# Splitting the first small load of a bf16 layer-scale kernel in two

## The chip, the core and the metric

The kernel runs on one core of one Trainium2 chip. The time is device microseconds of that core, the median over several executions. Smaller is better.

## What is computed

The reference adds a scaled tensor to another one; the scale is one vector over the last dimension:

```python
B, S, D = 1024, 16, 512          # x, y: (B, S, D) bf16; gamma: (D,) bf16
def reference(x, y, gamma):
    return x + gamma * y
```

x, y and the output have 16,384 rows of 512 elements, 1 KB each. So 33.55 MB are read and 16.78 MB written, with one multiply and one add for each element.

## The kernel before

The 16,384 rows are laid over the 128 partitions, 128 rows to each. `BLOCKS = [8, 60, 60]` cuts these 128 rows into three blocks; within a block every partition's rows lie one after the other in memory, so one load or store of a block moves 8 or 60 KB for each partition in one piece (`rows_of`). All of y stays on chip in `y_sb`; the multiply and the add both write in place there, and the stores read from it. x has a smaller buffer, `x_sb`, of 75 rows: the last number of an x load says where in it the rows go. Rows 68 to 127 of x are put at row 15, over rows 23 to 67, and rows 0 to 7 at row 0, over rows 8 to 15, so these two loads wait until the adds that used the rows before are done.

The order of the work is written out by hand in three lists:

- `SP`: the loads of x and y, as (tensor, first row, end row, place). SyncE issues them in this order on one DMA queue (called q1 in the profile). `EARLY` moves the first two loads to the head of the program.
- `ACT`: gamma and the three stores, issued by ScalarE on another queue (q10). The stores are for rows 8 to 67, 68 to 127, and 0 to 7.
- `DVE`: what VectorE does. `PIECES = [8, 15, 45, 60]` cuts the 128 rows into pieces 0 to 3, and ('m', c) multiplies piece c of y by gamma (L170), ('a', c) adds piece c of x to it (L179). Piece 0 is the small block, pieces 1 and 2 together are rows 8 to 67, piece 3 is rows 68 to 127.

The function `ring` walks through a queue's list and puts a wait on the adds in front of an item that needs one. A wait holds everything behind it in the same list.

gamma is spread over the partitions at the start: TensorE multiplies a column of ones with the gamma row (L144), VectorE copies the product from PSUM (L146), and every multiply reads that copy.

No store starts while the big loads run. `RELEASE` names the load of rows 68 to 127 of x. TensorE waits for it and then raises two semaphores, one for ScalarE's first store and one for VectorE's add of piece 3:

```python
_take(s_load[RELEASE], 16, nc.tensor)
nc.tensor.sem_inc(s_go, 1)
nc.tensor.sem_inc(s_rel, 1)
```

A store also waits until the pieces of its rows are added (`s_add`, counted in the order of the adds in `DVE`). In front of a multiply or an add VectorE takes the semaphores of the loads that its piece needs and that it has not taken yet (`need`).

Of the kernel before, what the change touches and what calls it, by code (L numbers as in the profile page):

```python
# [9 lines left out]


SP = [
    ('y', 0, 8),
    ('y', 8, 68),
    ('x', 8, 68, 0),
    ('y', 68, 128),
    ('x', 68, 128, 15),
    ('x', 0, 8, 0),
]
ACT = [('g',), ('s', 8, 68), ('s', 68, 128), ('s', 0, 8)]  # L20
# [2 lines left out]

RELEASE = ('x', 68, 128, 15)

DVE = [('m', 0), ('m', 1), ('m', 2), ('a', 2), ('a', 1), ('m', 3), ('a', 3), ('a', 0)]
MULT, ADD = mybir.AluOpType.mult, mybir.AluOpType.add


# [6 lines left out]
def kernel(  # L36
# [49 lines left out]
    s_add, s_go, s_rel, s_end, s_out = sem("s_add"), sem("s_go"), sem("s_rel"), sem("s_end"), sem("s_out")  # L86
    added = [a for kind, *a in DVE if kind == "a"]
    order = {a[0]: k for k, a in enumerate(added)}
# [74 lines left out]

    for kind, *args in DVE:
        c = args[0]
# [58 lines left out]
```

## Time and profile before

| what | value |
|---|---|
| time, median of 3 runs (lowest to highest) | 119.93 us (119.85 to 120.49) |
| span of the profiled execution | 118.5 us |
| VectorE busy | 70.1 us (59%) |
| TensorE busy | 0.6 us |
| load queue q1 | 33.55 MB, 65.8% of 16 engines' span |
| gamma and store queue q10 | 16.78 MB, 32.7% |
| multiply of piece 0, add of piece 0 | 2.29 us, 2.28 us |
| multiply, add of piece 3 | 16.16 us, 16.16 us |

The span is counted from the first to the last instruction of the profiled execution; the time takes in a little more. L33 is the helper `_take`, so a wait that ends with DVEq L33 is one for a semaphore of VectorE's own list. In the lines of the profile DVE is VectorE, PE is TensorE, SPq and ACTq are the DMA issues of SyncE and ScalarE. A line of the timeline has the start, the length up to the end of the last instruction merged into it, engine, line, operation, output and input, how many there are, and in brackets how long the engine stood idle before it and what ended that. A line of a stretch has its window and length, then the busy time of PE, PEld, DVE and POOL, the granted clock, the share of the DMA engines, and GB/s.

### The profile page before, as it was taken

The page shows a single profiled execution, that of the slowest core. Times are in us where ns is not written, and L with a number is a line of the kernel's source. Part 1 is how long each engine was busy: PE and PEld are TensorE (multiplying, and loading weights), DVE is VectorE, ACT ScalarE, POOL GpSimd, SP SyncE. Part 2 cuts the span into 40 slices and gives each one's busy share as a digit, 9 for nine tenths or more (in the row PEclk, how much of TensorE's full clock was granted, in tenths as well). Part 3 has the DMA queues.
Part 4 walks back from the last instruction along what each step waited for, and adds up shares of the span by engine and source line. Part 5 has one row for each costly group of instructions (what it writes and reads, how often), then busy time and mean ns, then how long its engine had stood idle before and what let it go on. Part 6 is the DMA issues. An engine that isn't in the chain of part 4 may idle for free. (4 is left out here: it accounts for less than half of the span.)

```text
span 118.5 us, 81 instructions
## 1 busy us (share of the span) xinstructions
PE 0.6 (0%) x1; PEld 0.1 (0%) x1; DVE 70.1 (59%) x10; POOL 0.2 (0%) x4
## 2 busy tenths in 40 slices
PE   0001000000000000000000000000000000000000
PEld 0000000000000000000000000000000000000000
DVE  0005400299999399999499999469999950000000
POOL 0000000000000000000000000000000000000000
DMA  5999779779779779978977977897797797797787
GB/s 180 506 602 394 332 332 663 332 332 663 332 332 663 332 332 601 394 332 352 643 332 332 663 332 332 384 633 332 332 663 332 332 663 332 332 663 332 332 365 321
DMA packets 1298, 50.33 MB, mean 425 GB/s; under 512 B 145, under 2 KB 146, under 8 KB 146
## 3 DMA queue, kind: packets, MB, share of 16 engines
q1 hardware_dynamic: 864, 33.55, 65.8%
q10 hardware_dynamic: 434, 16.78, 32.7%
HBM read 33.56 MB, written 16.78 MB: 425 GB/s over the span
## 5 line engine op out<-in xcount | busy, mean ns | idle before, releaser
L170 DVE TENSOR_TENSOR y_sb<-y_sb,gamma_sb 128x4096 bf16<-128x4096 bf16 (+3 forms) x4 | 34.7, 8689 | 11.9 <-DVEq L33 11.9
L179 DVE TENSOR_TENSOR y_sb<-x_sb,y_sb 128x23040 bf16<-128x23040 bf16 (+3 forms) x4 | 34.6, 8688 | 4.5 <-DVEq L33 4.5
L146 DVE CAST gamma_sb<-gamma_ps 128x512 bf16<-128x512 f32 x1 | 0.7, 690 | 7.9 <-DVEq L33 7.9
L141 DVE MEMSET ones_row<- 1x128 bf16 x1 | 0.2, 165 | 2.0 <-PEq L49 2.0
L144 PE MATMUL gamma_ps<-gamma_row,ones_row 1*128 1x512 bf16 x1 | 0.6, 581 | 9.3 <-PEq L33 9.3
L144 PEld LDWEIGHTS gamma_ps<-gamma_row,ones_row 1*128 1x128 bf16 x1 | 0.1, 97 | 9.3 <-issue 9.3
L208 POOL MEMSET const-bfloat16-1.0<- 128x1 bf16 x1 | 0.1, 102 | 0.0
L208 POOL MEMSET const-uint8-127<- 128x1 uint8 x1 | 0.1, 102 | 0.0
L208 POOL MEMSET const-float32-0.0<- 128x1 f32 x1 | 0.1, 99 | 0.2 <-issue 0.2
L208 POOL MEMSET const-float32-1.0<- 128x1 f32 x1 | 0.1, 99 | 0.0
## 6 DMA issues: line engine op xcount, KB each, us to landing
y_sb<-in_y_dram SPq DMA_DIRECT2D x2, 7680.0 KB, 39.8
x_sb<-in_x_dram SPq DMA_DIRECT2D x2, 7680.0 KB, 31.5
out_dram<-y_sb ACTq DMA_DIRECT2D x2, 7680.0 KB, 21.0
y_sb<-in_y_dram SPq DMA_DIRECT2D x1, 1024.0 KB, 4.8
x_sb<-in_x_dram SPq DMA_DIRECT2D x1, 1024.0 KB, 22.3
out_dram<-y_sb ACTq DMA_DIRECT2D x1, 1024.0 KB, 22.1
gamma_row<-in_gamma_dram ACTq DMA_DIRECT2D x1, 1.0 KB
```

The costliest lines, as they stand in the source:

```text
L141: nc.vector.memset(ones_row, 1.0).then_inc(s_ones, 1)
L144: nc.tensor.matmul(gamma_ps, ones_row, gamma_row, start=True, stop=True).then_inc(s_ps, 1)
L146: nc.vector.tensor_copy(out=gamma_sb, in_=gamma_ps).then_inc(s_dve, 1)
L170: nc.vector.tensor_tensor(out=yt, in0=yt, in1=g, op=MULT).then_inc(s_dve, 1)
L179: nc.vector.tensor_tensor(out=yt, in0=xt, in1=yt, op=ADD).then_inc(s_add, 1)
L208: nc = _bacc.Bacc("TRN2", target_bir_lowering=False, num_devices=1)
```

## The change

The load of rows 0 to 7 of y, the first of all, is cut in two. Rows 0 to 3 stay in first place; rows 4 to 7 go behind the last big load, in front of the small load of x. The aim is that rows 8 to 67 of y, with which the long work of VectorE begins, reach the chip earlier. Since the whole of piece 0 is then on chip only near the end of the loads, its multiply goes from first place in VectorE's list to the last but one.

```diff
 SP = [
-    ('y', 0, 8),
+    ('y', 0, 4),
     ('y', 8, 68),
     ('x', 8, 68, 0),
     ('y', 68, 128),
     ('x', 68, 128, 15),
+    ('y', 4, 8),
     ('x', 0, 8, 0),
 ]
-DVE = [('m', 0), ('m', 1), ('m', 2), ('a', 2), ('a', 1), ('m', 3), ('a', 3), ('a', 0)]
+DVE = [('m', 1), ('m', 2), ('a', 2), ('a', 1), ('m', 3), ('a', 3), ('m', 0), ('a', 0)]
```

## The prediction

> **What bounds the kernel now.** I read the slices of the page first, then the same stretch summed over the whole stream, then the timeline and the chain of waits. The page's slices show which resource is never idle:
>
> ```profile
> DVE  0005400299999399999499999469999950000000
> ...
> DMA  5999779779779779978977977897797797797787
> ...
> DMA packets 1298, 50.33 MB, mean 425 GB/s; under 512 B 145, under 2 KB 146, under 8 KB 146
> ...
> q1 hardware_dynamic: 864, 33.55, 65.8%
> q10 hardware_dynamic: 434, 16.78, 32.7%
> ```
>
> VectorE is idle for whole stretches; the DMA row never falls to 0, and the two queues together fill 98.5% of 16 engines' span. q1 is the load queue (SyncE issues it), q10 gamma and the stores (ScalarE). The sevens are no gaps: bytes and time are booked in coarse packets of up to 61,440 B. Over the stream from its first packet to its last the share is
>
> ```profile
> 1.00:118.20 117.20, 0.58 (x1) 0.10 (x1) 70.12 (x10) 0.00 (x0) 1.00 1.00 429
> ```
>
> The last two columns are the share of the DMA engines, 1.00, and 429 GB/s. The trace's packet records say it packet by packet: a 61,440 B packet takes 2.267 us, an 8,192 B one 0.309 us, the next one on the same engine starts within 0.05 us, and no longer gap is found on any engine between 1.03 us (first packet) and 118.11 us (last end). So the kernel lasts as long as its bytes, plus a start of about 1.8 us and a tail of 0.4 us for the last landing. The timeline shows where the order of work could leave a hole:
>
> ```profile
> 0.00 0.85 SPq L130 DMA_DIRECT2D y_sb<-in_y_dram  x2
> 1.90 0.33 SPq L127 DMA_DIRECT2D x_sb<-in_x_dram  x1
> ...
> 11.02 2.29 DVE L170 TENSOR_TENSOR y_sb<-y_sb,gamma_sb 128x4096 bf16<-128x4096 bf16 x1 [0.26 <-DVEq L33]
> 23.10 16.23 DVE L170 TENSOR_TENSOR y_sb<-y_sb,gamma_sb 128x7680 bf16<-128x7680 bf16 x2 [9.79 <-DVEq L33]
> 41.36 16.23 DVE L179 TENSOR_TENSOR y_sb<-x_sb,y_sb 128x23040 bf16<-128x23040 bf16 x2 [2.04 <-DVEq L33]
> 53.55 4.39 SPq L127 DMA_DIRECT2D x_sb<-in_x_dram  x2
> 59.40 16.16 DVE L170 TENSOR_TENSOR y_sb<-y_sb,gamma_sb 128x30720 bf16<-128x30720 bf16 x1 [1.81 <-DVEq L33]
> 77.76 19.02 ACTq L133 DMA_DIRECT2D out_dram<-y_sb  x3
> 78.05 18.36 DVE L179 TENSOR_TENSOR y_sb<-x_sb,y_sb 128x30720 bf16<-128x30720 bf16 x2 [2.49 <-DVEq L33]
> ```
>
> The reader is to see that each VectorE stage ends with a wait of 1.8 to 9.8 us for a load, so VectorE follows the loads, and that its work is issued to the queues ahead of need. The load of x rows 68 to 127 is issued at 53.55, 5.0 us before its first packet runs (58.55). The second store is issued at 94.24, 3.0 us before the first store's packets end (97.27). The chain that ended last says the same by what it lacks:
>
> ```profile
> by line: issue 12.0%; DVE y_sb L179 3.5%
> ...
> 79.94 14.18 issue
> 94.13 2.28 DVE y_sb L179
> ```
>
> It goes back only from the last store's issue through the last two adds; the 22 us behind 96.4 are stores, which it doesn't count as work.
>
> **What the Trainium skill says.** "DMA: Bandwidth & Descriptors", section "Where 436 GB/s comes from", gives 435.2 GB/s for the 16 ports together. The trace agrees: 61,440 B in 2.267 us is 27.1 GB/s per engine, 433.6 for sixteen. Only fewer bytes, or less start and tail, would make the kernel faster, and the change touches no byte count. The same page, "Queues, rings and completion order", says that an engine round-robins between queues packet by packet. The trace shows one case: the 1 KB packet of gamma (q10, issued at 1.91) ran at 6.56 between two 61,440 B packets of q1, and its semaphore write came one such packet later, at 8.87. The same page, "Latency and other measured facts", prices an HBM access at 0.2 us on average; the trace of before has no store-to-load change on an engine, so this is used below as a price. "VectorE: DVE Perf Modes", section "The perf-mode tier table", has bf16 tensor_tensor at 1224 ns for 2048 elements, so a moved instruction keeps its price; here 4096 elements take 2.29 us.
>
> **The change, part by part.**
> *The load stream.* One load of 8 packets of 8,192 B per engine becomes two of 8 packets of 4,096 B. From the two packet sizes: 53,248 B cost 1.958 us, so 27.19 B per ns and 7.7 ns fixed. A 4,096 B packet is then 0.158 us by that estimate, 16 of them 2.53 us against 8 x 0.309 = 2.47: +0.06 us. One semaphore write more per engine is 0.009 us. Both lie on the stream, and so on the end: +0.07.
> *The start.* Before, first packets begin at 1.03 to 1.83 and all end by 2.28, the earliest taking 1.04 us: cold latency. Then come seven more, until 4.20. Now eight short ones take 8 x 0.151 = 1.21 us less, so with the 0.07 of the next item they end from 3.06 on, and rows 8 to 67 of y must be queued by then. That load is issued at 0.43; with the first load's delay of 1.03 to 1.83 it is there at 1.46 to 2.26, so 0.8 us to spare. If the cold latency ends with one packet in flight, it now hides 0.15 us less data: 0 to 0.15, I take 0.07.
> *VectorE.* Multiply 0 (2.29 us) leaves a place where VectorE then idled 9.79 us, which hid it, and goes between add 3 and add 0, with a wait for two y loads that landed long before. All big loads land 1.14 us earlier (1.21 less 0.07): rows 8 to 67 of y at 21.8 for 22.96, the last big x load at 76.3 for 77.41. Add 3 starts near 76.9 and ends near 93.1, multiply 0 at 95.4, add 0 at 97.7, against 96.42. Behind multiply 0 only add 0 is queued, and for that waits only the last store, issued near 97.8. It is next in its queue when the second store ends, at about 115.5, and needs some 1.4 us from issue to packets (77.76 to 79.14 for the first store): 16 us of room. Cost 0. The second store is issued at 93.1 in place of 94.2; its room grows.
> *The hand-over from loads to stores.* Stores are released when the last big x load lands. Before, 2.47 us of x rows 0 to 7 ran behind that load: the first store was issued at 77.76, and its packets began at 79.14, on each engine straight after the last load packet. Now 1.27 us of y rows 4 to 7 run there too. The first store is issued near 76.6 and is ready from 77.6 (1.03 later) to 78.0 (1.4 later), with 4 to 6 load packets and semaphore writes left on q1. Taken in turn with 61,440 B store packets, x rows 0 to 7 land after about 79.2 + 5 x 2.27 + 0.35 = 90.9 (0.35: from a last packet to its landing, as 4.20 to 4.54); at worst, with 7 left, 95.4. Add 0 needs them at 95.4, and has 16 us beyond. So no engine idles, and the order of packets leaves the sum as it is. What is unknown is whether an engine loses time where a load follows a store. Lower bound: nothing, as at the load-to-store change (0.01 us). Upper: 5 x 0.2 = 1.0 us by the skill's HBM price, or 5 x 0.73 = 3.7 us with the cold latency of the first packet (1.04 less 0.31). I take 0.02 each, 0.1 in all: packets of one queue follow each other without any exposed latency, so reads are asked for ahead. Gamma points there too: with the store's 1.4 us it was ready at 3.3, yet three 8 KB packets and one big one of q1 went first. If that is look-ahead, there are hardly any alternations at all.
> Sum: 0.07 + 0.07 + 0 + 0.1 = +0.24; half of the last two is guesswork, so 119.93 + 0.2 = 120.1 us.
>
> **Rivals.**
> A, slower by the mixed queues: each of 5 alternations exposes a read, 1.0 us by the price in place of the 0.1 taken, so 121.0; up to 123.7 with the cold latency. For it: the kernel has never mixed small loads with stores in this trace, and the end is set by every lost engine nanosecond. Against: the look-ahead above.
> B, slower by a hole at the start: if rows 8 to 67 of y were ready only at 4.20, where they start now, 1.1 us are lost: 120.1 + 1.1 = 121.2. For it: nothing in the trace shows them ready earlier. Against: issue times and the first load's delay put them at 2.3.
> C, faster: data earlier on VectorE and an earlier store shorten the end. VectorE does get its inputs 1.14 us sooner, and if that reached the end the time would be 118.8. Against: the stores have no hole to close, the first follows the loads at once and the second is queued 3 us ahead. Known savings end at a shorter cold start, some 0.3 us, so this case would need something that the trace doesn't show.
>
> **How the numbers follow.** The forecast (a stream as long as before, 119.9 to 120.4) has 0.70. A has 0.17 and B 0.05, C 0.08, of which 0.07 pass the 0.5% bound of 0.6 us. Slower by over 0.5% means above 120.53: A and B, all but a little, 0.23 with the tail of the forecast; same 0.70. The range of 119.7 to 121.2 holds the forecast with the spread of the runs before (119.85 to 120.49), B, and A by the price; left out are C and A's high end.
>
> **What would show it.** Right: packets of 4,096 B near 0.158 us, no gap on an engine at 3.1 us, the big y load landing near 21.8, the release near 76.3, first store issued near 76.6, x rows 0 to 7 landing as late as 91, multiply 0 after add 3 without a wait, and the last packet near 118.3. Wrong: a hole at 3.1 us (B), load packets that take clearly over 0.31 us or follow a store with a gap (A), or a last store that starts after a hole because add 0 came too late, past 114.

## The result, and the profile after

The changed kernel takes 121.01 us (120.98 to 121.26, 6 runs) beside 119.94 us before: a ratio of 1.0088, with a 95% interval of 1.0068 to 1.0109. It is slower by 1.1 us. The profiled execution of it is the longest of its six, 121.26 us with a span of 119.9 us; the other five have spans of 119.7 to 119.8.

The page's slices, with the packets and the queues:

```profile
DVE  0001000399999399999399999199999980000000
...
DMA  5997997998998998998999899698997998998975
...
DMA packets 1442, 50.33 MB, mean 420 GB/s; under 512 B 161, under 2 KB 162, under 8 KB 418
...
q1 hardware_dynamic: 1008, 33.55, 65.6%
q10 hardware_dynamic: 434, 16.78, 32.3%
```

The bytes are the same, and the engines still never rest for a slice. Only the mean rate is lower, 420 for 425 GB/s. The last two slices are emptier than before (7, 5 where there was 8, 7): some engines finish before others. So the time is lost somewhere inside a stream that looks busy all along. The timeline shows where it is not lost:

```profile
22.90 16.23 DVE L171 TENSOR_TENSOR y_sb<-y_sb,gamma_sb 128x7680 bf16<-128x7680 bf16 x2 [10.81 <-DVEq L34]
...
59.22 16.16 DVE L171 TENSOR_TENSOR y_sb<-y_sb,gamma_sb 128x30720 bf16<-128x30720 bf16 x1 [1.82 <-DVEq L34]
77.56 21.46 ACTq L134 DMA_DIRECT2D out_dram<-y_sb  x3
77.86 16.16 DVE L180 TENSOR_TENSOR y_sb<-x_sb,y_sb 128x30720 bf16<-128x30720 bf16 x1 [2.48 <-DVEq L34]
93.93 2.29 DVE L171 TENSOR_TENSOR y_sb<-y_sb,gamma_sb 128x4096 bf16<-128x4096 bf16 x1
96.37 2.29 DVE L180 TENSOR_TENSOR y_sb<-x_sb,y_sb 128x4096 bf16<-128x4096 bf16 x1
```

Multiply 0 and add 0 follow add 3 with no bracket behind them, so they wait for no load. Add 0 ends at 98.7, and the last store has until the second one ends, past 115. But the first line is at 22.90 where it was 23.10: cutting 0.5 MB from the head of the queue brought the long work forward by 0.2 us and not by 1.1. So the loss is at the head. Stretches of the start (same columns as the stretch shown in the prediction), first before:

```profile
1.00:2.20 1.20, 0.00 (x0) 0.00 (x0) 0.17 (x1) 0.00 (x0) 1.00 0.79 205
2.20:2.80 0.60, 0.00 (x0) 0.00 (x0) 0.00 (x0) 0.00 (x0) 1.00 0.97 410
```

and after:

```profile
1.00:2.20 1.20, 0.00 (x0) 0.00 (x0) 0.17 (x1) 0.00 (x0) 1.00 0.91 218
2.20:2.80 0.60, 0.00 (x0) 0.00 (x0) 0.00 (x0) 0.00 (x0) 1.00 0.76 191
```

Up to 2.2 us the two are alike. Then before goes to its full rate, and after stays at half of it. The view books a packet where it starts; cut to the stretch, the packet records fill 0.99 of the 16 engines between 2.2 and 2.8 us. So no engine waits for work: what is long is the packets themselves. The records give 4,096 B packets of 0.261 us on average at the start (up to 0.768), and of 0.162 in the late load. The first y load lands on the engines from 3.31 to 4.51 us, where it had been 4.54 to 4.82. The spread over the engines stays: 1.20 us at this landing, 1.10 at that of the last big x load, 1.38 at the end. The time at which each transfer's last engine landed, from the trace's landings, in us:

```
                     before   after   difference
y rows 0 to 7 / 3      4.82    4.51     -0.31
y rows 8 to 67        22.96   22.76     -0.20
last big x load       77.41   77.22     -0.19
y rows 4 to 7          -      78.72   (+1.50 behind the line above)
x rows 0 to 7         79.90   81.19     +1.29
first store           98.00   99.36     +1.36
last store           118.50  119.90     +1.40
```

The last engine saved 0.2 us at the front and paid for the other half of the bytes at the back in full (1.28 us by 0.159 a packet; on the 0.22 beyond that see the swapped halves below).

### The profile page after: what moved, and what is told of

The parts are those of the page before. It is cut to its first block, busy times and chain, and to the rows that moved or that the text cites. A ratio compares the mean times of both kernels' runs of the same rounds, so it can differ in the third digit from the quotient of the medians.

```text
span 119.9 us, 84 instructions
## 1 busy us (share of the span) xinstructions
PE 0.6 (0%) x1; PEld 0.1 (0%) x1; DVE 70.1 (58%) x10; POOL 0.2 (0%) x4
## 5 line engine op out<-in xcount | busy, mean ns | idle before, releaser
L171 DVE TENSOR_TENSOR y_sb<-y_sb,gamma_sb 128x7680 bf16<-128x7680 bf16 (+3 forms) x4 | 34.7, 8688 | 12.6 <-DVEq L34 12.6
```

The source lines that it names most:

```text
L171: nc.vector.tensor_tensor(out=yt, in0=yt, in1=g, op=MULT).then_inc(s_dve, 1)
```

## The experiments

Two theories at first: S, the start (the small packets on cold queues, that is on queues that have just begun, put the engines out of step), and L, the late load (rows 4 to 7 at the back, and the stores that meet them).

**The split alone** (e1_split_first), from the kernel before:

```diff
-    ('y', 0, 8),
+    ('y', 0, 4),
+    ('y', 4, 8),
     ('y', 8, 68),
-EARLY = (2, 0)
+EARLY = (3, 0)
```

> Both halves of y's small block are loaded first, one after the other, and the multiply of piece 0 stays in first place: the split alone, without the late load. Theory S (start): packets of 4,096 B on cold queues put the engines out of step, as in the changed kernel, where they ended the first load from 2.98 to 4.16 us; the slowest one then needs 8 x 0.159 more, ends near 5.4 in place of 4.43, and the whole is slower by about 1.0 us: 120.9. Theory L (late load): the loss comes from rows 4 to 7 behind the big loads, and from the stores that meet them; then this kernel costs only 0.07 us for its smaller packets: 120.0.

It took 120.78 us (120.73 to 120.85), ratio 1.0072 (1.0060 to 1.0085). No load was moved to the back, so 0.87 of the 1.1 us belong to the front, as S has it. The stretches of its start show something more:

```profile
2.20:3.00 0.80, 0.00 (x0) 0.00 (x0) 0.17 (x1) 0.00 (x0) 1.00 0.87 200
3.20:4.20 1.00, 0.00 (x0) 0.00 (x0) 0.00 (x0) 0.00 (x0) 1.00 1.03 418
```

The first half runs at 200 GB/s, and the second, with the same 4,096 B packets, at 418 (0.168 us a packet on average). The size of the packets is not what is slow. Nor is a distance of 8 KB from one partition to the next enough, for the second half has it too; it lies beside the rows that the first half has just read.

**The late load alone** (e2_late_only), from the changed kernel:

```diff
-    ('y', 0, 4),
-    ('y', 8, 68),
+    ('y', 8, 16),
+    ('y', 0, 4),
+    ('y', 16, 68),
```

> The queue starts with rows 8 to 15 of y in packets of 8,192 B; rows 0 to 3 come second, and rows 4 to 7 late as in the changed kernel: the late load alone, without 4,096 B packets on cold queues. S: the engines stay within 0.3 us of each other, 120.0 to 120.2. L: as slow as the changed kernel, 121.0.

It took 120.54 us (120.53 to 120.56), ratio 1.0052 (1.0038 to 1.0065), which neither theory gave. The stretches, of rows 0 to 3 of y in second place and of rows 4 to 7 late:

```profile
4.40:5.80 1.40, 0.00 (x0) 0.00 (x0) 0.00 (x0) 0.00 (x0) 1.00 0.87 278
76.00:76.80 0.80, 0.00 (x0) 0.00 (x0) 0.00 (x0) 0.00 (x0) 1.00 0.99 405
```

Rows 0 to 3 are slow in second place too, though less (0.196 us a packet on average, 73 of the 128 at the full rate), and the queues had been running at 420 from 2.2 to 3.0 us. That moves S from "cold queues" to that load itself. The late half is at full rate. From the last big x load to the end it is 42.42 us here and 41.09 before: 1.33 more. The late half's own 8 packets of 0.159 are 1.27 of that, bytes that left the front, so the late place costs 0.06.

**The halves without holes** (e3_contiguous), from the changed kernel:

```diff
     def rows_of(t, a, b):
+        if t is yf and b <= 8:
+            return t[P * a : P * b].rearrange("(p n) d -> p n d", p=P)
```

> As the changed kernel, but y's rows 0 to 3 are read as one unbroken stretch of memory, and rows 4 to 7 as the next one, in place of 4 KB out of every 8 KB (so piece 0 multiplies other rows of y than those that belong to it). S by holes: if it is the pitch that slows the first packets, the first load now ends evenly near 3.1 to 3.3 us and the time is 120.1. S by count or size of packets: 121.0, with the same spread of the first load. L: 121.0.

It took 120.37 us (120.17 to 120.55), between the two. The first load lands from 2.88 to 3.41, and the last big x load at 76.01, which is 1.40 us earlier than before and more than the 1.14 that were forecast. In the profiled execution, the longest of its five, x rows 0 to 7 then took 3.19 us for 2.49:

```profile
77.80:78.80 1.00, 0.00 (x0) 0.00 (x0) 1.00 (x1) 0.00 (x0) 1.00 1.07 287
```

That is another fall of the rate, in a load of whole 8,192 B packets, and in most other runs it is not there.

**The block cut by partitions** (e4_half_partitions), from the changed kernel:

```diff
-    ('y', 0, 4),
+    ('y', 0, 8, 0),
...
-    ('y', 4, 8),
+    ('y', 0, 8, 64),
...
+                ps = slice(w[3], w[3] + 64) if len(w) > 3 else slice(0, P)
-                i = eng.dma_start(out=y_sb[:, r, :], in_=rows_of(yf, w[1], w[2])).then_inc(s_load[w], 16)
+                i = eng.dma_start(out=y_sb[ps, r, :], in_=rows_of(yf, w[1], w[2])[ps]).then_inc(s_load[w], 16)
```

> As the changed kernel, but the block is cut by partitions: rows 0 to 7 of partitions 0 to 63 first, those of 64 to 127 late. Per engine 4 packets of 8,192 B in place of 8 of 4,096 B, the same bytes. S by count, size or holes: first load even, ended near 3.1 to 3.3, 120.0 to 120.2. If the start has a stretch of low rate that passes at a fixed time, whatever the packets are, the first load ends late and unevenly here too: 120.6 to 121.0. L: 121.0.

It took 122.28 us (122.19 to 122.48), and tells nothing about the theories: all expectations missed a cost of its own. The late half alone took 2.34 us, nearly as much as the whole block before (2.49), at half rate:

```profile
77.40:79.20 1.80, 0.00 (x0) 0.00 (x0) 0.95 (x1) 0.00 (x0) 1.00 1.05 218
```

The Trainium skill, "SBUF — State Buffer", section "Door 1: The DMA port swizzle", says that the rate of a DMA depends on how many of the 16 ports its partitions reach, and its table puts partitions 64 to 127 on eight of them. The measured 218 GB/s, half of the full rate, agrees.

**The halves swapped** (e7_swap): ('y', 4, 8) first and ('y', 0, 4) late.

> As the changed kernel with the halves swapped: rows 4 to 7 of y first, rows 0 to 3 late. Theory T (first): whichever half comes first on the small block loses its rate at the start; 121.0, first load ended unevenly near 3.0 to 4.2 us, late half at 0.159 us a packet. Theory A (address): rows 0 to 3 are slow wherever they stand; then the first load ends evenly near 3.1, the late one has packets far over 0.159 us, and the time is other than 121.0 by over 0.3 us.

It took 121.37 us (121.00 to 121.63). Its profiled execution, of 121.00 us, has the first load landing from 3.33 to 4.54, and all 128 late packets at 0.159 us: whichever half comes first is the slow one (T). Here the late half took the expected 1.28 us, and the end came at 119.65. So the 0.22 more that the profiled execution of the changed kernel spent on its late half is not a part of the usual loss. Two of its three other executions took over 121.6, longer than any of the changed kernel; where they lost that is not known.

**Other distances between partitions** (e9_pitch12, e9_pitch16, e9_pitch24), from the changed kernel; 12 stands for the number of rows, 1 KB each:

```diff
     def rows_of(t, a, b):
+        if t is yf and b <= 8:
+            return t[: P * 12].rearrange("(p n) d -> p n d", p=P)[:, a:b, :]
```

> As the changed kernel, but the two halves of y's small block are read from memory with 12 KB from one partition to the next in place of 8 KB (so piece 0 multiplies other rows of y than those that belong to it). Theory P (pitch): it is the pitch of 8 KB, a power of two, with half of it read, that brings the rate of the start down to about 200 GB/s; with 12 KB the first load ends by 3.4 and the time is 120.0 to 120.5. Theory H (holes): any pitch that leaves holes does it; 121.0.

> The same with 16 KB from one partition to the next (again other rows of y in piece 0). P: a power of two, so slow at the start as the changed kernel, 121.0. H: 121.0 too. If it is as fast as 12 KB, neither a power of two nor a hole is the cause, and 8 KB is a case of its own.

> As the run with 12 KB, with 24 KB between partitions (again other rows of y in piece 0). If a power of two is what matters: fast start, 120.0 to 120.4. If every multiple of 8 KB is slow: 120.8 to 121.1.

With 12 KB: 120.15 us (120.07 to 120.56, 14 runs), ratio 1.0023 (1.0015 to 1.0031). With 16 KB: 120.88 (120.86 to 121.65). With 24 KB: 120.38 (120.26 to 120.71), ratio 1.0046 (1.0032 to 1.0059). The same stretch of the start, with 12 KB:

```profile
2.20:2.80 0.60, 0.00 (x0) 0.00 (x0) 0.00 (x0) 0.00 (x0) 1.00 1.01 416
```

and with 16 KB:

```profile
2.20:2.80 0.60, 0.00 (x0) 0.00 (x0) 0.00 (x0) 0.00 (x0) 1.00 0.78 212
```

Both read 4 KB and leave a hole, so a hole by itself is not the cause; for the load at the front the distance decides. 24 KB is a multiple of 8 KB, and its time is nearer to that of 12 KB than to those of 8 and 16; its first load lies between, with 0.96 us from the first engine's landing to the last's for 0.53 (12 KB) and 1.17 (16 KB). The chip is no rival: the swapped halves, with 8 KB, were slow on the chip on which 12 KB was fast, and the late half from x below was so on the chip of 24 and 68 KB. With 12 KB the last big x load lands at 76.31, near the 76.3 of the prediction.

**All of y's small block late** (e5_all_late), from the changed kernel: ('y', 0, 4) is taken out and ('y', 4, 8) becomes ('y', 0, 8).

> No small load stands at the start: rows 8 to 67 of y first, in packets of 61,440 B, and all of rows 0 to 7 of y late, in front of those of x. The start can then lose nothing to small packets: engines within 0.3 us of each other after the first big load. If the start is the whole loss: 119.9 to 120.1. If small loads that run while the stores are issued lose time as the run with the unbroken halves showed (0.72 us for x rows 0 to 7): 120.4 to 120.7.

It took 120.98 us (120.79 to 121.18), ratio 1.0088 (1.0074 to 1.0102): slower than either expectation. A start in packets of 61,440 B loses little: the last big x load lands at 75.17, 2.24 us earlier, for the 2.47 us of bytes that went behind it. The packets of y rows 0 to 7 run at the full rate behind it (0.311 us on average, first line). The rest of the loss is in the packets of x rows 0 to 7 (0.417 on average for 0.309, 0.86 us over eight), while the first store is queued:

```profile
74.50:76.50 2.00, 0.00 (x0) 0.00 (x0) 0.68 (x1) 0.00 (x0) 1.00 1.02 430
77.00:79.00 2.00, 0.00 (x0) 0.00 (x0) 2.00 (x1) 0.00 (x0) 1.00 0.96 254
```

x rows 0 to 7 landed from 80.42 to 87.41, so some engines did take store packets in turn with them. The long packets all begin before 79.9; the six that run behind a store packet (from 81.93 on) begin within 0.02 us of its end and take 0.309 us. So the turns themselves cost nothing, and nor does the delay: add 0 ended at 96.6, long before its store's turn.

**68 KB between partitions, with the right rows** (f2_after_68, f1_before_68): BLOCKS = [68, 60] for [8, 60, 60], in the changed kernel and in the one before.

> The changed kernel with BLOCKS = [68, 60] in place of [8, 60, 60]: rows 0 to 67 of a partition lie together, so every small load and store has 68 KB from one partition to the next, and the loads and the order are the same. Theory P (the pitch slows the first load): first load ended by 3.4 us on all engines, time 120.0 to 120.3, as with 12 KB. If the lateness has to do with small packets at the start after all: 120.8 to 121.1.

> The kernel before with the same BLOCKS = [68, 60]. P: its first load has packets of 8,192 B without holes and was not slow, so nothing changes but the spread of its times: 119.8 to 120.0. If the 68 KB were a gain by themselves, that would be seen here: under 119.7.

The changed kernel then takes 120.34 us (120.14 to 120.42), ratio 1.0036 (1.0024 to 1.0049), and the kernel before 119.92 (119.82 to 120.06), ratio 1.0004 (0.9996 to 1.0012). Nothing but the layout differs from the changed kernel, and 0.67 of its 1.07 us are gone; the expectation of 120.0 to 120.3 was a little low. The first load lands from 3.12 to 3.82, so a spread of 0.70 us is still there.

**A late half from memory not yet read** (e10_late_fresh), from the changed kernel:

```diff
-in_=rows_of(yf, w[1], w[2])
+in_=rows_of(xf if w[:2] == ('y', 4) else yf, w[1], w[2])
```

> The changed kernel with its late half read from the small block of x in place of y, at the same 8 KB pitch: memory that no load has read before, where the late half of y lies beside rows that have been read (piece 0 gets x in place of rows 4 to 7 of y). If a first reading of such a block is what is slow, its packets now take far over 0.159 us, and the time rises by 0.5 to 1.0 us, to 121.5 to 122.0. If the place at the start is what makes it slow: packets of 0.159 us, 121.0.

It took 121.21 us (120.96 to 121.56), ratio 1.0112 (1.0093 to 1.0130). In the profiled execution, the longest, its late packets took 0.179 us on average, for 0.162 in the changed kernel and 0.196 in second place in the run of the late load alone. But 108 of the 128 took 0.159. The 20 longer ones all begin from 77.28 on, when other engines were already at the next load, which reads the same block of x (from 77.01). So a first reading is not enough to make such a load slow; whether it has a part in it is not settled.

No version beat the kernel before.

## Why the prediction was right or wrong

Slower, which is what came, had a chance of 0.23, and no change had 0.70. The forecast's 120.1 us was 0.9 short. The range held the time, but by luck: its upper end stood there for rivals A and B, and neither of their mechanisms came.

The step that failed is *The start*, and in it the term "eight short ones take 8 x 0.151 = 1.21 us less". It took 4,096 B packets at 0.158 us, from the two sizes that the trace of before shows. They do take 0.159, but late (all 128 in five runs). At the start of the changed kernel they take 0.261 on average. A part of that is the cold latency, which the prediction had counted: before, it raised the mean of the first load's packets from 0.309 to 0.355, and the same 0.046 would make 0.204 of 0.158 (with 12 KB it is 0.194). The rest, 0.057 a packet or 0.46 us over eight, was not foreseen, and nor was that the engines share it unevenly. The big y load starts from 3.00 on the first engine to 4.16 on the last, for 4.20 to 4.43 before; the forecast said from 3.06 on. The last engine gained 0.20 us for 1.14, and the 0.94 between them are most of the 1.07. The two sizes priced a packet by its bytes and left out where in memory it begins. The distances of 12, 24 and 68 KB show that this matters: they take back 0.6 to 0.9 us.

One reading in that step is a little off: the earliest packet begins at 1.04 us and took 1.11, where the prediction has 1.04. This changes only an upper bound of the hand-over, 4.0 us for 3.7.

*The load stream*, +0.07: right by the late packets (0.159 against 0.158).

*VectorE*, cost 0: right. Multiply 0 starts at 93.93 without a wait, and the last store is issued at 98.69, with more than 16 us to spare. The big loads came only 0.2 us earlier, but nothing rests on that.

*The hand-over*: no alternation in the changed kernel. The store packets begin on each engine from 79.38 to 80.87, after that engine's last x packet, so x rows 0 to 7 landed at 81.19 and not near 91. The first store was issued 1.0 us later than forecast, and the look-ahead was the better reading for this kernel. The all-late run shows the turns between queues that the Trainium skill describes ("DMA: Bandwidth & Descriptors", section "Queues, rings and completion order"). But both it and the run without holes show small loads falling to 254 to 287 GB/s, and that was in no step. Their long packets begin 1.27 and 1.36 us after the first store's issue, which is about when its packets are ready (1.38 in the trace of before). With 12 KB no packet there is long, so the store alone does not bring it about; the cause was not sought. Whether it is the cause of the slow start too is not known.

Rival A, an exposed read at each change of queue, did not happen: in the changed kernel there were no such changes, and in the all-late run a load packet behind a store packet took its 0.309 us. Rival B had nearly the size (121.2) with a wrong mechanism: rows 8 to 67 of y were there at 3.00, and from 2.2 to 2.8 us the engines were full. Rival C fell on its own ground: even with the full 1.40 us gained at the front (the run without holes), the time was 120.37.

What is left with 12, 24 and 68 KB, 0.25 to 0.48 us, is partly the +0.07; for 12 KB the trace gives the rest: 1.10 us gained of 1.21, 1.25 paid for the late half, 0.06 more in the first store, in sum +0.21 at the end. A start in 4,096 B packets leaves a spread of 0.5 to 1.0 us over the engines in all of these runs, where 8,192 B ones left 0.28, and 0.42 with 68 KB.

Open: why a distance of 8 KB halves the rate at the front, and lowers it to 278 GB/s in second place, and not in the same load late, which ran at 0.159 us in run after run. The place in the queue alone isn't the answer, for in the run of the split alone the other half of the same 8 KB ran at the full rate in second place. The engines' step alone isn't it either: with rows 8 to 15 of y in front, they were 0.4 us apart at the slow load and at the fast one. The Trainium skill, "DMA: Bandwidth & Descriptors", section "Latency and other measured facts", tells of copies whose rate falls from 207 GB/s with 512 KiB from one partition's row to the next to 103 with 4 MiB, and is back at 214, the full one there, with 4 KiB more; it names aliasing of memory channels as an unverified inference. Here, too, the distance decides and not the bytes, but at 8 and 16 KB; whether the mechanism is the same was not tried.

## What to carry to other kernels

Where the stream of transfers is full, moving a load within it gains nothing, and the question is only what each packet costs in its new form and place. A packet's price from two sizes held for a third one (53,248 B took 1.97 us in the run of the late load alone, as the two sizes give) and for 4,096 B late. It did not hold for half of every 8 KB read at the head of the queue, which ran at 191 GB/s where whole 8 KB ran at 410. Look at the last engine's landing, not at the mean: a spread that arose in the first 4 us was still there at the end.

## What the runs showed that was not expected

- The rate of a load of 4 KB pieces over 128 partitions depended on the distance between them: at the front, from 2.2 to 2.8 us, 191 GB/s with 8 KB, 212 with 16, 416 with 12.
- The same load with 8 KB ran at 0.159 to 0.162 us a packet behind the big loads, and at 0.168 right behind its other half.
- A load of 64 partitions took 2.34 us for 0.5 MB, near the 2.49 us of 128 partitions and 1 MB.
- Contiguous small loads of 8,192 B packets fell to 254 to 287 GB/s for 1 to 2 us in two of the runs, and stayed at 433 (77.4 to 78.8 us) in the kernel before.
- Load packets that ran behind a store packet on the same engines took no longer than others, 0.309 us for 8,192 B (six of them, in one run).
